# A provisional softmax bound for the first 512 keys of an attention block, with one input block transposed by DMA

## The chip, the cores and the metric

The kernel runs on one core of a Trainium2 chip. The metric is the device time of one execution in microseconds. A core has a matrix engine (TensorE, "PE" in the profile; its weight loads are "PEld"), a vector engine (VectorE, "DVE"), a scalar engine (ScalarE, "ACT"), GpSimd ("POOL") and SyncE ("SP"), which here only issues DMA transfers. DMA issues on the queue of an engine stand under "SPq" or "ACTq".

The profiled span is a little shorter than the reported time (413.1 against 415.36 us for the same execution of the kernel before). Reported times are compared with reported times, and points inside the span with points inside the span.

## The reference

```python
# x (1, 2048, 448), wqkv (448, 1344), wo (448, 448), all bf16;  H = 16 heads of Dh = 28
qkv = (x @ wqkv).reshape(B, S, 3, H, Dh).transpose(2, 0, 3, 1, 4)
q, k, v = qkv
scores = einsum("bhqd,bhkd->bhqk", q, k) * Dh ** -0.5
p = softmax(scores)
o = einsum("bhqk,bhkd->bhqd", p, v)
out = o.transpose(0, 2, 1, 3).reshape(B, S, D) @ wo
```

## The kernel before

**Shape of the work.** Four heads form a group, each padded from 28 to 32 rows of the 128 partitions. The queries come in chunks of 512. So there are 4 groups x 4 chunks = 16 windows; each window has 16 key tiles x 4 heads = 64 score tiles of 128 keys x 512 queries, 1024 in all. A score tile takes one matmul, then an exponential, and then one matmul into the value sums in the PSUM bank PO. Two engines make exponentials: ACT takes two tiles at once as one 128x1024 activation (848 tiles, 424 activations), and DVE with GpSimd takes 176 tiles with a polynomial (three DVE passes, one GpSimd pass).

**The bound.** Softmax needs something like the row maximum of the scores. The kernel uses an upper bound instead: the sum over d of |q_d| times the largest |k_d| over all keys. It comes out of the score matmul itself: next to the 32 rows of a head stand 32 more rows, which hold |q| on the query side (QB) and minus 1.03 times the maximum of |k| on the key side (KB). No exponential can start until the maximum over *all* 2048 keys is known, so until all four x blocks are loaded, transposed and projected to keys.

```python
    for b in range(NQC):                       # four x blocks of 512 rows
        nc.sync.dma_start(out=XS[b][:], in_=x_perm[:, b * TPC:(b + 1) * TPC, :])
    for (W, off) in ((WK, D), (WQ, 0)):
        nc.scalar.dma_start(out=W[:, :, 0:GW], in_=wq3[:, :, off:off + GW])
    ...
    for b in range(NQC):
        xs_in = add(Op("SP", 0.01, None, prio=-2000 + b, lat=(4.7, 6.1, 7.6, 9.0)[b]))
        for hf in range(2):
            ...
            tro = add(Op("PE", 0.55, tr, deps=[xs_in], ...))      # 8 transposes of 128x112 on TensorE
            evo = add(Op("DVE" if hf == 0 else "ACT", 0.6 if hf == 0 else 0.905, ev, deps=[tro], ...))
    ...
    def task_K(g, sc):                         # keys of block sc, group g
        ...
        if g == 0:
            red = ... tensor_reduce(out=KPART[g][:, sc:sc + 1], in_=ap(), op=ALU.max, apply_absolute_value=True)
            evs = [... nc.scalar.activation(out=KB[0][pr][:, cs], in_=ap(), func=ACT.Identity, bias=onescol[:, 0:1]) ...]
    def task_kmax(g):                          # maximum over the four blocks, then into the bound rows of KB
        m = ... tensor_reduce(out=KMAX[g][:], in_=KPART[g][:], op=ALU.max)
        ...
```

**The planner.** The kernel fixes the instruction order of each engine when it is built. A small event simulation in Python holds operations (`Op`: engine, assumed duration, assumed latency, dependencies, priority) and a handful of tuned constants, plays them through and emits the instructions in the order it finds. An engine then works through its list in that order. So an `Op("SP", 0.01, None, lat=4.7)` is an *assumption* that a load lands at 4.7 us. If it lands later on the chip, the result stays correct, but what stands behind its first user in that engine's order waits too: in the changed kernel below a block landed at 24.80 us where 13.0 was assumed, and score matmuls waited 8.9 us behind two projection matmuls that read it. The constants that matter below are `DI` (how many DVE tiles must be in work before output sums may go ahead of score matmuls near the end), `NTAIL` (DVE takes none of the last so many tiles), `UO` and `UQ` (how early a projection may take a bank from the score tiles), and `QEA`, `QPR`, `OD` for the order of the query projections.

## Time and profile before

The median of the three runs given with the kernel was 415.18 us (414.97 to 415.36).

| kernel before | us |
|---|---|
| first exponential starts | 16.38 |
| fourth exponential starts | 19.45 |
| last exponential ends | 405.56 |
| span ends | 413.1 |

From the page of the kernel before: its span, the busy time of each engine with its share of the span, and the chain of work that ended last, by engine.

```profile
span 413.1 us, 7525 instructions
PE 362.4 (88%) x2605; PEld 121.4 (29%) x2617; DVE 394.0 (95%) x696; ACT 400.0 (97%) x439; POOL 224.1 (54%) x203
ACT 86%; issue 8%; PE 2%; DMA 2%; DVE 1%; SPq 0%; DVEq 0%; ACTq 0%
```

ACT is busy for 97% of the span and makes up 86% of the chain that ended last: it bounds the kernel. DVE at 95% is close behind.

The timeline of ACT in the kernel before gives the start, in us from the start of the span, the length, and the instruction with the shapes written and read; in brackets stands the idle time before it and what ended that.

```profile
16.38 1.02 ACT L903 ACTIVATE PTA_131<-PA_198 128x1024 bf16<-128x1024 f32 x1 [0.25 <-PE PA_198 L631]
17.63 1.02 ACT L903 ACTIVATE PTA_132<-PA_199 128x1024 bf16<-128x1024 f32 x1 [0.23 <-PE PA_199 L631]
18.55 1.02 ACT L903 ACTIVATE PTA_133<-PA_198 128x1024 bf16<-128x1024 f32 x1
19.45 1.03 ACT L903 ACTIVATE PTA_134<-PA_199 128x1024 bf16<-128x1024 f32 x1
...
404.28 1.28 ACT L903 ACTIVATE PTA_145<-PA_199 128x1024 bf16<-128x1024 f32 x1
```

After the second exponential no line carries a bracket until the last one ends at 404.28 + 1.28 = 405.56. The 424 exponentials follow each other at 0.917 us. So the time is a start (16.4 us), a stretch of exponentials at full rate (389 us) and a tail (7.5 us).

The timeline of DVE in the kernel before shows what stands in the tail.

```profile
400.13 0.69 DVE L727 SCALAR_TENSOR_TENSOR PTD_162<-PD_200,DG_182 128x512 uint16<-128x512 f32 x1 [0.50 <-POOL DG_182 L714]
403.58 0.63 DVE L602 TENSOR_TENSOR XS_129<-PD_202,KB_0_91 128x448 bf16<-128x448 f32 x1 [2.76 <-PE PD_202 L598]
...
406.04 0.72 DVE L643 STREAM_TRANSPOSE DT<-PO 128x512 f32<-128x512 f32 x1
```

DVE's last polynomial tile is finished at 400.82, 4.7 us before ACT's last exponential, so the last normalisation (the transpose of PO into DT) can start at 406.04, 0.5 us after that exponential.

### The profile page before, as it was taken

The page shows a single profiled execution, that of the slowest core. Times are in us where ns is not written, and L with a number is a line of the kernel's source. Part 1 is how long each engine was busy: PE and PEld are TensorE (multiplying, and loading weights), DVE is VectorE, ACT ScalarE, POOL GpSimd, SP SyncE. Part 2 cuts the span into 40 slices and gives each one's busy share as a digit, 9 for nine tenths or more (in the row PEclk, how much of TensorE's full clock was granted, in tenths as well). Part 3 has the DMA queues.
Part 4 walks back from the last instruction along what each step waited for, and adds up shares of the span by engine and source line. Part 5 has one row for each costly group of instructions (what it writes and reads, how often), then busy time and mean ns, then how long its engine had stood idle before and what let it go on. Part 6 is the DMA issues. An engine that isn't in the chain of part 4 may idle for free.

```text
span 413.1 us, 7525 instructions
## 1 busy us (share of the span) xinstructions
PE 362.4 (88%) x2605; PEld 121.4 (29%) x2617; DVE 394.0 (95%) x696; ACT 400.0 (97%) x439; POOL 224.1 (54%) x203
## 2 busy tenths in 40 slices
PE   8988989898898889888898988979898888989995
PEld 4533232223232232322223222222322222222231
DVE  6899999999999999999999999999999999999975
ACT  4999999999999999999999999999999999999994
POOL 2155456464655556475465656547375656556450
PEclk9999999999999999999999999999999999999999
DMA  8410011202201001110400001010310101001012
GB/s 256 77 20 21 3 47 11 53 25 54 72 1 44 2 28 30 20 38 8 111 8 27 21 9 40 2 36 11 77 48 2 47 2 35 12 27 47 4 69 89
DMA packets 33413, 15.83 MB, mean 38 GB/s; under 512 B 26016, under 2 KB 30304, under 8 KB 33376
## 3 DMA queue, kind: packets, MB, share of 16 engines
q1 hardware_dynamic: 32304, 15.05, 14.5%
q8 instruction: 20, 0.33, 0.4%
q10 hardware_dynamic: 1072, 0.32, 0.3%
q14 instruction: 17, 0.14, 0.1%
HBM read 7.37 MB, written 1.96 MB: 23 GB/s over the span
## 4 chain that ended last, share of the span: by engine, by line
ACT 86%; issue 8%; PE 2%; DMA 2%; DVE 1%; SPq 0%; DVEq 0%; ACTq 0%
ACT PTA_131 L903 5%; ACT PTA_132 L903 4%; ACT PTA_133 L903 4%; ACT PTA_136 L903 4%; ACT PTA_135 L903 4%; ACT PTA_134 L903 4%; ACT PTA_145 L903 4%; ACT PTA_140 L903 4%; ACT PTA_139 L903 4%; ACT PTA_138 L903 4%; ACT PTA_137 L903 4%; ACT PTA_144 L903 4%; ACT PTA_142 L903 3%; ACT PTA_143 L903 3%; ACT PTA_141 L903 3%
## 5 line engine op out<-in xcount | busy, mean ns | idle before, releaser
L714 POOL TENSOR_TENSOR DG_181<-DV_175,DU_169 128x512 f16<-128x512 f16 x30 | 34.6, 1155 | 34.8 <-DVE DV_175 L711 34.6
L714 POOL TENSOR_TENSOR DG_182<-DV_176,DU_170 128x512 f16<-128x512 f16 x30 | 34.6, 1155 | 28.8 <-DVE DV_176 L711 28.7
L714 POOL TENSOR_TENSOR DG_184<-DV_178,DU_172 128x512 f16<-128x512 f16 x29 | 33.5, 1155 | 29.5 <-DVE DV_178 L711 28.2
L714 POOL TENSOR_TENSOR DG_186<-DV_180,DU_174 128x512 f16<-128x512 f16 x29 | 33.5, 1155 | 26.9 <-DVE DV_180 L711 26.7
L714 POOL TENSOR_TENSOR DG_185<-DV_179,DU_173 128x512 f16<-128x512 f16 x29 | 33.5, 1155 | 25.7 <-DVE DV_179 L711 25.6
L714 POOL TENSOR_TENSOR DG_183<-DV_177,DU_171 128x512 f16<-128x512 f16 x29 | 33.5, 1156 | 22.9 <-DVE DV_177 L711 22.7
L631 PEld LDWEIGHTS <-KB_1_94 64*128 64x128 bf16 x256 | 20.8, 92 | 48.4 <-issue 47.4
L631 PEld LDWEIGHTS <-KB_0_91 64*128 64x128 bf16 x256 | 20.5, 92 | 45.8 <-issue 42.1
L631 PEld LDWEIGHTS <-KB_1_92 64*128 64x128 bf16 x256 | 20.1, 93 | 45.8 <-issue 44.0
L631 PEld LDWEIGHTS <-KB_0_93 64*128 64x128 bf16 x256 | 20.3, 92 | 43.5 <-issue 42.5
L903 ACT ACTIVATE PTA_140<-PA_199 128x1024 bf16<-128x1024 f32 x18 | 22.4, 1247 | 0.0
L903 ACT ACTIVATE PTA_144<-PA_199 128x1024 bf16<-128x1024 f32 x18 | 22.4, 1245 | 0.0
L903 ACT ACTIVATE PTA_143<-PA_198 128x1024 bf16<-128x1024 f32 x18 | 22.3, 1241 | 0.0
L903 ACT ACTIVATE PTA_142<-PA_199 128x1024 bf16<-128x1024 f32 x18 | 22.3, 1239 | 0.0
L903 ACT ACTIVATE PTA_141<-PA_198 128x1024 bf16<-128x1024 f32 x18 | 22.3, 1236 | 0.0
L903 ACT ACTIVATE PTA_139<-PA_198 128x1024 bf16<-128x1024 f32 x17 | 21.1, 1241 | 0.0
L708 DVE TENSOR_SCALAR DU_171<-PD_202 128x512 f16<-128x512 uint16 x29 | 19.8, 682 | 1.0 <-PE PD_202 L631 0.7
L708 DVE TENSOR_SCALAR DU_172<-PD_200 128x512 f16<-128x512 uint16 x29 | 19.7, 681 | 0.9 <-PE PD_200 L631 0.9
L711 DVE SCALAR_TENSOR_TENSOR DV_178<-PD_200,DU_172 128x512 f16<-128x512 uint16 x29 | 19.8, 684 | 0.3
L711 DVE SCALAR_TENSOR_TENSOR DV_176<-PD_201,DU_170 128x512 f16<-128x512 uint16 x29 | 19.8, 683 | 0.2
L708 DVE TENSOR_SCALAR DU_169<-PD_200 128x512 f16<-128x512 uint16 x29 | 19.8, 682 | 0.2 <-PE PD_200 L631 0.2
L903 ACT ACTIVATE PTA_145<-PA_198 128x1024 bf16<-128x1024 f32 x16 | 20.0, 1247 | 0.0
(596 smaller groups left out, 1511.3 us busy)
## 6 DMA issues: line engine op xcount, KB each, us to landing
RRB_194<-SCR_196 SPq DMA_DIRECT2D x8, 256.0 KB
RRB_195<-SCR_197 SPq DMA_DIRECT2D x7, 256.0 KB
KB_1_94<-KB_0_93 SPq DMA_DIRECT2D x4, 128.0 KB
XS_127<-in_x_dram SPq DMA_DIRECT2D x1, 448.0 KB
XS_128<-in_x_dram SPq DMA_DIRECT2D x1, 448.0 KB
XS_129<-in_x_dram SPq DMA_DIRECT2D x1, 448.0 KB
XS_130<-in_x_dram SPq DMA_DIRECT2D x1, 448.0 KB
out_dram<-XS_127 SPq DMA_DIRECT2D x1, 448.0 KB
```

The source lines that it names most:

```text
L631: nc.tensor.matmul(out=ap, lhsT=KB[g % 2][i // 2][a:a + 64, j * P:(j + 1) * P], rhs=QB[w % NQB][i // 2][a:a + 64, :], start=True, stop=Tru ...
L708: p1 = add(Op("DVE", P1, lambda: nc.vector.tensor_scalar(out=DU[b][:], in0=lo, scalar1=SIG / 65536, scalar2=SIG * (SS - 0.5), op0=ALU.mult ...
L711: p2 = add(Op("DVE", P1, lambda: nc.vector.scalar_tensor_tensor(out=DV[b][:], in0=lo, scalar=65536 * (SS - 0.5 + CE / C3), in1=DU[b][:], o ...
L714: gq = add(Op("POOL", PTT, lambda: nc.gpsimd.tensor_tensor(out=DG[b][:], in0=DV[b][:], in1=DU[b][:], op=ALU.mult), deps=[p2], prio=n, kind ...
L903: nc.scalar.activation(out=PTA[pslot.idx][:, 0:len(ns) * QW], in_=PA[s.idx][:, 0:len(ns) * QW], func=ACT.Exp, bias=ACT_BIAS, scale=ACT_SCALE)
```

## The change

The intent is to start the exponentials earlier. The first 512 keys of the first window get a bound of their own, from the maximum of their own block. Only x block 0, WK and WQ are needed for it. The other 1536 keys of that window use the bound of all keys, as before. The two partial value sums then stand on different bases: the first is multiplied by the exponential of the difference of the bounds (8 small matmuls, one 128x512 activation on ACT, one multiplication on GpSimd) and added to the second at the end of the window.

Four further parts go with it:
- For group 0 the maximum moves from the key side to the query side (a DVE multiplication for each query chunk), and the keys of blocks 1 to 3 are copied to their places by eight DMA moves.
- Constants are made on GpSimd, which is idle for 6.38 us up to 8.75 in the trace of the kernel before, and partly on DVE. WQ goes to the sync queue right after x block 0, and WO is loaded later.
- One of the four x blocks (rows 8 to 11 of every 16) is not transposed on TensorE any more but loaded by 16 transposing DMAs of 128x128.
- The planner's constants are set anew.

The diff, cut to its core (most of it left out, marked by `...`):

```diff
-    DI = 2
+    DI = 1
-    QEA = 30
+    QEA = 20
-    UQ = 16
-    OD = 4
+    UQ = 30
+    OD = 2
-    UO = 40
+    UO = 20
+    FB = TPC
+    XLAT = (4.45, 6.9, 8.3, 9.6)
+    WQLAT = 5.9
+    XT3 = 13.0
+    T0 = (0, 4, 12, 8)
...
+    nc.scalar.dma_start(out=WK[:, :, 0:GW], in_=wq3[:, :, D:D + GW])
     for b in range(NQC):
-        nc.sync.dma_start(out=XS[b][:], in_=x_perm[:, b * TPC:(b + 1) * TPC, :])
-    for (W, off) in ((WK, D), (WQ, 0)):
-        nc.scalar.dma_start(out=W[:, :, 0:GW], in_=wq3[:, :, off:off + GW])
+        if b < NQC - 1:
+            nc.sync.dma_start(out=XS[b][:], in_=x_perm[:, T0[b]:T0[b] + TPC, :])
+        if b == 0:
+            nc.sync.dma_start(out=WQ[:, :, 0:GW], in_=wq3[:, :, 0:GW])
     nc.sync.dma_start(out=WV[:], in_=wq3[:, :, 2 * D:3 * D])
+    for cc in range(CC):
+        for t in range(TPC):
+            nc.sync.dma_start(out=XT[NQC - 1][cc // 2][:, cc % 2, t * P:(t + 1) * P],
+                              in_=bass.AP(x.tensor, x.offset + (T0[NQC - 1] + t) * D + cc * CK, [[NKT * D, P], [1, P]]),
+                              transpose=True)
...
+    xt_done[NQC - 1].append(add(Op("SP", 0.01, None, prio=-1996, lat=XT3)))
+    add(Op("SP", 10.2, None, prio=-1995.5))
...
+            b0 = []
             for i in range(HG):
...
+                o = bound(qb, i, KPART[0], [ab, kmaxop[0][0], e1], -4370 + 0.01 * i if i < 2 else -4350 + 0.01 * i)
+                b0.append(o)
                 qev[(g, c, i)] = [o]
+            for i in range(HG):
+                qev2[i] = bound(q2, i, KMAX[0], [cps[i // 2], ab, kmax_op[0]], -4000 + 0.01 * i)
...
-                         rhs=QB[w % NQB][i // 2][a:a + 64, :], start=True, stop=True, tile_position=(a, 0))
+                         rhs=QB[2 if w == 0 and j >= FB else w % NQB][i // 2][a:a + 64, :], start=True, stop=True, tile_position=(a, 0))
...
+    def task_factor():
+        ...
+        e = add(Op("ACT", 0.49, lambda: nc.scalar.activation(out=DT[:], in_=bank(task)[:], func=ACT.Exp, scale=ACT_SCALE),
+                   deps=[m], prio=0))
...
+    def finish_block():
+        pvop = rows[(0, FB - 1)]["pv"]
+        ev = add(Op("DVE", 0.62, lambda: nc.vector.tensor_copy(out=RRB[1][:], in_=PO[:]), deps=[pvop], prio=-5000))
+        ...
+        first_part.append(add(Op("POOL", 1.22, lambda: nc.gpsimd.tensor_tensor(out=RRB[1][:], in0=RRB[1][:], in1=DT[:], op=ALU.mult),
+                                 deps=[ev, factor], prio=-10, kind="n")))
```

`XT3 = 13.0` and the 10.2 below it are the planner's assumptions about the transposing DMAs: all landed at 13.0 us, the sync queue busy until about 10.2 us. The 10.2 count from the start of the simulation, because the operations before it on that queue take 0.01 us each.

## The prediction

One sentence is cut out of the text below, where marked. It was no term of the forecast's sum (net 2.2 to 2.7 us, 412.5 us), which stands in full.

> **What bounds the kernel now.** ScalarE (ACT). By the page, ACT is busy 97% of the 413.1 us span, VectorE (DVE) 95%; the chain that ended last is 86% ACT, nearly all 128x1024 exponentials. By the timeline the first exponential starts at 16.38, and from the second on ACT has no idle gap until the last ends at 405.56: 424 exponentials in 389.2 us, 0.917 apart. The other 176 score tiles take three DVE passes and one GpSimd pass each. So the time is 16.4 us of start, 389 of exponentials, 7.5 of tail.
>
> **What sets the 16.4 us.** By the timeline: WQ is padded only from 8.75 (GpSimd, 1.33 us); four x blocks are transposed on TensorE and copied by ACT (1.0 us) and DVE (0.69 us); four key projections, four DVE maxima (0.69 us) and the overall maximum (14.21) precede the bound; the query is projected last (13.2), evacuated at 14.29; bounds and absolute values end at 15.8.
>
> **What the change does.** The first 512 keys need only x block 0, WK, WQ and their own maximum. ACT loses two copies (1.0 us each) before the first exponential and evacuates query and keys sooner; two key evacuations move to after the third exponential. One x block comes by 16 transposing DMAs from the sync queue. GpSimd makes constants in idle time. The instruction orders show the same 424 exponentials and 176 DVE tiles, so the 389 us term stays.
>
> Estimate from trace durations: x block 0 lands about 4.6, is transposed and copied by 7.1; query and key matmuls end by 8.7; ACT query evacuation to 9.6; DVE absolute value, copy, x-copy (0.69) and two bounds (0.72) end near 11.5; first exponential near 12.0, 4.4 us earlier. Given back on ACT later: two key evacuations (0.59 us pitch, 1.2 us), one 128x512 exponential for the factor (0.5 us), and a 0.5 us gap before the second exponential (one buffer, second pair of bounds). Net 2.2 to 2.7 us. Added DVE work after the start (three multiplies of 0.25, one 0.68 us evacuation, more bounds) is off the chain, but DVE has only a few us of idle between 17 and 400.
>
> **Prediction: 412.5 us, 80% range 410.3 to 414.6.** Faster by over 2%: 0.03; within 2%: 0.95; slower by over 2%: 0.02.
>
> **What would show it.** Timeline: first exponential at 11.5 to 12.8; the fourth (before: 19.45) near 16.5; spacing 0.917 afterwards; the last ending 2 to 3 us earlier; tail about 7.5 us. ACT waits under 1 us in total after the third exponential.
>
> **What would make it wrong.**
> - TensorE, in order, meets key block 3's matmuls before the second to fifth score groups. No DMA transpose is in this trace; if the last lands after about 15 us, every later exponential shifts. The kernel's plan assumes 13.0.
> - The eight moves of keys 512 to 2047 by DMA: an issue took 0.63 us before, and a tile waited until 1.6 us after the last issue. [...] My estimate: first needed about 20 us, the first four landing by 20: little slack, a 1 us stall is possible.
> - DVE starting its tiles later (near 19 against 17.35) with more work: if the balance tips, ACT or the tail waits.
> - Faster than I think: data lands earlier, or the retuned tail order saves some of the 7.5 us.

## The result, and the profile after

| | median us | lowest to highest | runs |
|---|---|---|---|
| before | 415.08 | 414.57 to 415.36 | 4 |
| after | 425.94 | 425.65 to 426.47 | 4 |

The ratio is 1.0268 (95% interval 1.0253 to 1.0282): slower. A ratio here and below is not quite the ratio of the medians that are quoted.

From the page of the changed kernel: span, busy times and the chain that ended last.

```profile
span 424.5 us, 7553 instructions
PE 361.5 (85%) x2593; PEld 121.0 (28%) x2606; DVE 396.6 (93%) x703; ACT 397.6 (94%) x436; POOL 229.0 (54%) x222
ACT 79%; issue 6%; PE 5%; SPq 5%; DVE 2%; DMA 1%; DVEq 0%
```

The engines do nearly the same work as before (ACT even 2.4 us less), but the span is 11.4 us longer: this is waiting. The new member of the chain is "SPq" with 5%, the issuing of DMAs on the sync queue.

The timeline of ACT in the changed kernel:

```profile
12.00 1.04 ACT L1047 ACTIVATE PTA<-PA 128x1024 bf16<-128x1024 f32 x1
13.54 1.94 ACT L1047 ACTIVATE PTA<-PA 128x1024 bf16<-128x1024 f32 x2 [0.49 <-PE PA L729]
15.86 0.69 ACT L467 ACTIVATE KB<-PD,onescol 128x512 bf16<-128x512 f32 x1 [0.38 <-DVE KPART L454]
26.28 0.69 ACT L467 ACTIVATE KB<-PD,onescol 128x512 bf16<-128x512 f32 x1 [9.74 <-DVE KPART L454]
26.87 3.83 ACT L1047 ACTIVATE PTA<-PA 128x1024 bf16<-128x1024 f32 x4
31.83 1.02 ACT L1047 ACTIVATE PTA<-PA 128x1024 bf16<-128x1024 f32 x1 [1.13 <-PE PA L729]
```

The first exponential starts at 12.00, 4.4 us earlier than before. Three run, and then ACT waits 9.74 us to evacuate the keys of the last x block. The line puts the wait down to DVE's maximum of that block (KPART), but DVE was itself idle for 9.73 us just then, waiting for the projection. So one looks one step further back, at the timeline of PE in the changed kernel:

```profile
15.07 0.39 PE L729 MATMUL PA<-QB,KB 64*128 64x512 bf16 x2
19.72 0.61 PE L447 MATMUL PD<-XT,WKP 112*128 112x512 bf16 x1 [4.26 <-DMA XT<-in_x_dram]
24.93 0.59 PE L447 MATMUL PD<-XT,WKP 112*128 112x512 bf16 x1 [4.60 <-DMA XT<-in_x_dram]
25.45 0.61 PE L729 MATMUL PA<-QB,KB 64*128 64x512 bf16 x2
```

In PE's order the last two matmuls of that projection (L447) stand between the score matmuls (L729). Each waits for transposed pieces of x, 8.9 us together, and the scores behind them wait too, although nothing that the next ones read is missing (e_true below ran five exponentials in this time). And the timeline of the sync queue in the changed kernel shows why the pieces are late:

```profile
3.20 20.48 SPq L235 DMA_TRANSPOSE XT<-in_x_dram  x16
```

The 16 transposing DMAs need from 3.20 to 23.68 only to be *issued*, 1.28 us apart. The chain shows the last one issued at 22.45 and landed 2.35 us later, at 24.80, where the plan had 13.0.

The windows view of the changed kernel adds the granted TensorE clock. After the stretch come its length, busy time and number of instructions for PE, PEld, DVE, ACT and POOL, then the clock, the DMA share and GB/s.

```profile
17.00:21.40 4.40, 0.61 (x1) 0.11 (x1) 0.00 (x0) 0.00 (x0) 0.00 (x0) 0.64 0.14 25
21.40:38.00 16.60, 11.04 (x80) 5.16 (x81) 10.99 (x21) 10.58 (x12) 3.38 (x3) 0.79 0.30 43
```

In the first of these stretches, inside TensorE's wait, its granted clock averages 0.64, and it averages 0.79 over the 16.6 us after that. Narrower windows of the same view show 1.00 from 15.46 to 18.00, 0.60 from 18 to 19, 0.50 from 19 to 28, 0.78 from 28 to 29 and 1.00 from 29 to 32, so the clock halved near 18.2 and came back near 28.4. The fall came about 2.7 us after the last matmul before the wait had ended (15.46), the return about 3.5 us after work resumed at 24.93. What decides these times was not shown.

The end of the changed kernel, in DVE's timeline and then in PE's:

```profile
413.29 0.68 DVE L861 SCALAR_TENSOR_TENSOR PTD<-PD,DG 128x512 uint16<-128x512 f32 x1
...
417.31 0.72 DVE L743 STREAM_TRANSPOSE DT<-PO 128x512 f32<-128x512 f32 x1 [2.27 <-PE PO L900]
```

```profile
414.33 1.88 PE L764 MATMUL PD<-WO,OT 128*128 128x448 bf16 x9
...
416.36 0.82 PE L900 MATMUL PO<-PTA,VA 128*32 128x512 bf16 x12
```

The last exponential ends at 414.73. DVE's last tile is finished at 413.97, only 0.76 us before it (4.7 us before, in the kernel before). Nine matmuls of the output projection stand in front of the last value matmuls, and the final normalisation starts at 417.31, 2.6 us after the last exponential instead of 0.5.

So the 11.4 us of longer span are, term by term:

| part of the span, us | before | after | difference |
|---|---|---|---|
| start to first exponential | 16.38 | 12.00 | -4.38 |
| first to fourth exponential | 3.07 | 14.87 | +11.80 |
| fourth exponential to the end of the last | 386.11 | 387.86 | +1.75 |
| end of the last exponential to the end | 7.54 | 9.77 | +2.23 |
| sum | 413.1 | 424.5 | +11.4 |

The 1.75 is made of the wait of 1.13 at 31.83 (score matmuls that wait for the key moves by DMA), 0.47 for the factor's activation (it starts at 43.59 in the same timeline, the next exponential at 44.06), and 0.15 that was not assigned.

### The profile page after: what moved, and what is told of

It is laid out like the page before. It is cut to its first block, busy times and chain, and to the rows that moved or that the text cites. A ratio compares the mean times of both kernels' runs of the same rounds, so it can differ in the third digit from the quotient of the medians.

```text
span 424.5 us, 7553 instructions
## 1 busy us (share of the span) xinstructions
PE 361.5 (85%) x2593; PEld 121.0 (28%) x2606; DVE 396.6 (93%) x703; ACT 397.6 (94%) x436; POOL 229.0 (54%) x222
## 4 chain that ended last, share of the span: by engine, by line
ACT 79%; issue 6%; PE 5%; SPq 5%; DVE 2%; DMA 1%; DVEq 0%
ACT PTA L1047 79%; SPq L235 4%; PE PA L729 2%; PE PO L900 1%; DMA KB<-KB 1%; DMA XT<-in_x_dram 1%; PE PO L550 0%; PE PD L764 0%; DVE DV L845 0%; PE PD L729 0%; SPq L229 0%; SPq L496 0%; DVE DU L842 0%; PE PO L447 0%; ACT OUTF L1176 0%
## 5 line engine op out<-in xcount | busy, mean ns | idle before, releaser
L1047 ACT ACTIVATE PTA<-PA 128x1024 bf16<-128x1024 f32 x424 | 389.5, 1252 | 1.6 <-PE PA L729 1.6
L848 POOL TENSOR_TENSOR DG<-DV,DU 128x512 f16<-128x512 f16 x176 | 202.3, 1153 | 176.7 <-DVE DV L845 169.0
L729 PE MATMUL PA<-QB,KB 64*128 64x512 bf16 x848 | 167.4, 381 | 44.3 <-ACT PTA L1047 40.4
L842 DVE TENSOR_SCALAR DU<-PD 128x512 f16<-128x512 uint16 x176 | 118.6, 680 | 3.5 <-PE PD L729 3.2
L729 PEld LDWEIGHTS <-KB 64*128 64x128 bf16 x1024 | 67.2, 93 | 186.0 <-issue 178.8
L845 DVE SCALAR_TENSOR_TENSOR DV<-PD,DU 128x512 f16<-128x512 uint16 x176 | 118.8, 681 | 1.1
L861 DVE SCALAR_TENSOR_TENSOR PTD<-PD,DG 128x512 uint16<-128x512 f32 x176 | 119.0, 678 | 0.6 <-POOL DG L848 0.2
L900 PE MATMUL PO<-PTA,VA 128*32 128x512 bf16 x848 | 85.6, 386 | 0.0
L729 PE MATMUL PD<-QB,KB 64*128 64x512 bf16 x176 | 65.1, 379 | 1.1 <-DVE PTD L861 0.4
L900 PE MATMUL PO<-PTD,VA 128*32 128x512 bf16 x176 | 58.1, 387 | 0.0
L447 PE MATMUL PO<-XT,WKP 112*128 112x512 bf16 x48 | 15.0, 385 | 0.1
L447 PE MATMUL PD<-XT,WKP 112*128 112x512 bf16 x16 | 5.4, 407 | 9.3 <-DMA XT<-in_x_dram 8.9
L454 DVE TENSOR_REDUCE KPART<-PD 128x1 f32<-128x512 f32 x4 | 2.8, 690 | 10.4 <-PE PD L447 10.3
L447 PEld LDWEIGHTS <-WKP 112*128 112x128 bf16 x64 | 4.6, 97 | 18.6 <-issue 13.3
```

Of the source, the lines that this page charges most:

```text
L447: ops = chain_mm(CC, lambda cc: nc.tensor.matmul(out=ap(), lhsT=WKP[g][:, cc, :], rhs=XT[sc][cc // 2][0:CK, cc % 2, :], start=(cc == 0), s ...
L729: nc.tensor.matmul(out=ap, lhsT=KB[g % 2][i // 2][a:a + 64, j * P:(j + 1) * P], rhs=QB[2 if w == 0 and j >= FB else w % NQB][i // 2][a:a + ...
L842: p1 = add(Op("DVE", P1, lambda: nc.vector.tensor_scalar(out=DU[b][:], in0=lo, scalar1=SIG / 65536, scalar2=SIG * (SS - 0.5), op0=ALU.mult ...
L845: p2 = add(Op("DVE", P1, lambda: nc.vector.scalar_tensor_tensor(out=DV[b][:], in0=lo, scalar=65536 * (SS - 0.5 + CE / C3), in1=DU[b][:], o ...
L848: gq = add(Op("POOL", PTT, lambda: nc.gpsimd.tensor_tensor(out=DG[b][:], in0=DV[b][:], in1=DU[b][:], op=ALU.mult), deps=[p2], prio=n, kind ...
L861: f = add(Op("DVE", P1, lambda: nc.vector.scalar_tensor_tensor(out=PTD[st["s"].idx][:].bitcast(U16), in0=PX[slot.idx][:], scalar=EBITS + C ...
```

## The experiments

**Theory**: the change loses because of the transposing DMAs. They are too many instructions for one queue, the plan believed that they land at 13.0, and everything behind their first user in PE's order waits. The gain of 4.4 us at the start is real. **Rival 1**: the new structure (bounds on the query side, key moves, factor, a second pass over PO) loses time by itself and would be slower with any loading of x. **Rival 2**: it is not the DMAs but the wrong plan; told the truth, the planner would find other work for the wait. Later a third question came up: what makes the tail longer. The expectations below name their alternatives each in its own words; where one speaks of a theory and a rival by letter or name, it means those stated in that text.

All kernels gave correct results. Times are medians in us. The kernel before had 414.78 (7 runs) in the rounds of the first four rows, 414.79 (7 runs) in those of the next four, and 414.95 (9 runs) in those of the last three.

| label | what it is | median | ratio (95%) |
|---|---|---|---|
| e_pe | change, last x block transposed on TensorE | 426.57 | 1.0284 (1.0269 to 1.0300) |
| e_before_dt | kernel before with the 16 transposing DMAs | 428.94 | 1.0347 (1.0324 to 1.0371) |
| e_big | change, 4 transposing DMAs instead of 16 | 415.60 | 1.0019 (1.0002 to 1.0036) |
| e_true | change, planner told the measured landing | 431.45 | 1.0400 (1.0384 to 1.0415) |
| e_pe2 | as e_pe, other bank for one transpose | 416.10 | 1.0029 (1.0014 to 1.0043) |
| e_after_di | change, only `DI` set back | 425.74 | 1.0263 (1.0245 to 1.0281) |
| e_big_di | e_big, `DI` set back | 414.65 | 0.9996 (0.9981 to 1.0011) |
| e_mid | change, 8 transposing DMAs | 415.52 | 1.0014 (0.9998 to 1.0031) |
| e_after_tail | change, two tiles fewer on DVE, `UO` set back | 424.82 | 1.0245 (1.0231 to 1.0260) |
| e_best | e_big with the tail of e_after_tail | 414.40 | 0.9987 (0.9974 to 1.0001) |
| e_pe_best | e_pe2 with its own tail | 414.34 | 0.9989 (0.9976 to 1.0002) |

### e_before_dt: the transposing DMAs alone, in the kernel before

```diff
+    XT3 = 13.0
+    T0 = (0, 4, 12, 8)
...
-    for b in range(NQC):
-        nc.sync.dma_start(out=XS[b][:], in_=x_perm[:, b * TPC:(b + 1) * TPC, :])
+    for b in range(NQC - 1):
+        nc.sync.dma_start(out=XS[b][:], in_=x_perm[:, T0[b]:T0[b] + TPC, :])
...
+    for cc in range(CC):
+        for t in range(TPC):
+            nc.sync.dma_start(out=XT[NQC - 1][cc // 2][:, cc % 2, t * P:(t + 1) * P], ..., transpose=True)
```

> The kernel before with only the 16 transposing DMAs put in for x block 3. Theory: the last transposed piece lands at 24.8, the first exponential moves from 16.4 to about 28 to 29.5, total 426 to 430 us. Rival (the transposing DMAs are harmless, the early bound is to blame): within 2 us of 415.

Measured: 428.94, a ratio of 1.0347; the DMAs alone cost 14 us, without any early bound. The timeline of ACT in this kernel:

```profile
25.89 0.69 ACT L399 ACTIVATE KB<-PA,onescol 128x512 bf16<-128x512 f32 x1 [11.57 <-DVE KPART L396]
28.99 3.77 ACT L914 ACTIVATE PTA<-PA 128x1024 bf16<-128x1024 f32 x4 [2.40 <-PE PA L642]
```

The first exponential moved from 16.38 to 28.99, with the same wait for the last key block. The total lies inside the expected 426 to 430, as the theory has it; rival 1 has no place for it. It is more than the change lost, because here no exponential can start before the last block has come.

### e_big and e_mid: fewer and larger transposing DMAs

The rows of a block are made consecutive in memory (the views of x and of the output change along), so that one DMA can transpose 512 or 256 rows. The diff of e_big against the changed kernel:

```diff
     for cc in range(CC):
-        for t in range(TPC):
-            nc.sync.dma_start(out=XT[NQC - 1][cc // 2][:, cc % 2, t * P:(t + 1) * P],
-                              in_=bass.AP(x.tensor, x.offset + (T0[NQC - 1] + t) * D + cc * CK, [[NKT * D, P], [1, P]]),
-                              transpose=True)
+        nc.sync.dma_start(out=XT[NQC - 1][cc // 2][:, cc % 2, :],
+                          in_=bass.AP(x.tensor, x.offset + T0[NQC - 1] * P * D + cc * CK, [[D, QW], [1, P]]),
+                          transpose=True)
```

e_mid takes two DMAs of 256 rows for each `cc`; apart from that it is e_big:

```diff
+        for hv in range(2):
+            nc.sync.dma_start(out=XT[NQC - 1][cc // 2][:, cc % 2, hv * 256:(hv + 1) * 256],
+                              in_=bass.AP(x.tensor, x.offset + (T0[NQC - 1] * P + hv * 256) * D + cc * CK, [[D, 256], [1, P]]),
+                              transpose=True)
```

> The change, but 4 transposing DMAs of 512 rows by 128 columns instead of 16 of 128 by 128 (rows of a block made contiguous so that one instruction can take them). Theory A (issue costs about 1.28 us per instruction): last landing near 9.5, fourth exponential near 16.5, total about 415 to 416 (the tail of the change, 2.2 us longer, stays). Theory B (issue costs per 128x128 piece, about 5 us per instruction): last landing near 25, total within 1.5 us of 425.9.

> Half-way dose: 8 transposing DMAs of 256 rows by 128 columns. Issue per instruction was 1.28 us at 128 rows and 1.8 us at 512, so 1.4 to 1.5 is expected here (mostly a cost per instruction), the queue free near 15, last landing near 16, fourth exponential at 18 to 19.5, total 416 to 418. If the cost were per byte: last landing near 25 and 425; but then 4 instructions would have cost that as well.

Measured: 415.60 and 415.52; e_big lies inside its expected range, e_mid just below its own. The three kernels asked for the line of their transposing DMAs (duration of one issue in ns as minimum/median/maximum, and the first and last start in us), first the changed kernel:

```profile
L235 SPq DMA_TRANSPOSE XT<-in_x_dram x16: 1215/1232/1352, 3.2 to 22.4; - x16
```

e_mid:

```profile
L235 SPq DMA_TRANSPOSE XT<-in_x_dram x8: 1240/1242/2244, 3.1 to 12.7; - x8
```

e_big:

```profile
L234 SPq DMA_TRANSPOSE XT<-in_x_dram x4: 1260/1720/2542, 3.1 to 9.3; - x4
```

An issue of 128 rows and one of 256 rows take the same 1.24 us (median), so in this range the cost goes by instruction and not by byte. At 512 rows the four issues of e_big took, in order, 2.54, 1.34, 2.10 and 1.26 us; the same four instructions took 1.91, 1.26, 1.39 and 1.26 in e_big_di. So the shortest issue is hardly longer than one of 128 rows, and the median of four says little. In e_mid too, the first and the last issue were longer than the rest (1.83 and 2.24). Whether the excess comes of the size or of a wait is not shown. The queue is free at 23.68 with 16 pieces, at 14.98 with 8, and at 10.53 with 4. In e_big nothing waits for the transposed block, in e_mid a matmul waits 0.7 us. One caution: the rows of a piece are 16 rows apart in memory in the changed kernel and consecutive in e_mid and e_big; e_mid's equal issue time speaks against that being the cause, but the two were not varied separately.

The timeline of ACT in e_big, to be held against that of the changed kernel:

```profile
12.69 1.04 ACT L1046 ACTIVATE PTA<-PA 128x1024 bf16<-128x1024 f32 x1
...
17.45 0.69 ACT L466 ACTIVATE KB<-PD,onescol 128x512 bf16<-128x512 f32 x1 [0.22 <-DVE KPART L453]
18.03 4.67 ACT L1046 ACTIVATE PTA<-PA 128x1024 bf16<-128x1024 f32 x5
```

The wait of 9.74 is now 0.22, and the fourth exponential starts at 18.03. (The first is 0.7 us later than in the changed kernel. In this execution x block 1 landed later: its transposes, which stand in PE's order before the query's projection, began at 7.68 against 7.00. In e_big_di, with the same start, the first exponential was at 11.67.) The change in the medians from 425.94 to 415.60 puts the price of the small pieces at 10.3 us. The theory holds for the main term. (e_mid's last piece landed at 16.14 and its fourth exponential started at 17.92, no later than in e_big, so its total is no worse either.) But e_big is not faster than the kernel before: the interval lies just above 1, so a rest was to be explained.

### e_pe and e_pe2: the last x block transposed on TensorE

Both take the transposing DMAs out and treat the fourth x block like the others. They differ in the PSUM bank of the block's first transposed half. e_pe:

```diff
-             ((PA[0][:, 0:QW], None), (PA[0][:, QW:2 * QW], None)), ())
+             ((PA[0][:, 0:QW], None), (PA[0][:, QW:2 * QW], None)), ((PO[:], 3), (PA[0][:, 0:QW], 4)))
...
-    open_when(o_slot, [xt_half[3]])
+    open_when(o_slot, [xt_half[6]])
```

> The change, but x block 3 loaded plainly and transposed on TensorE as before; early bound, rescaling and constants kept. Theory (the transposing DMAs on the sync queue cost the time: 16 issues of 1.28 us, last landing at 24.8): first exponential near 12, the fourth near 17 instead of 26.87, no wait over 1.5 us on ScalarE after it; total 411 to 414.5 us. Rival (the early bound with its second accumulation, factor, extra DVE passes and key moves costs the time): at least 420 us.

Measured: 426.57, as slow as the change. Taken alone this would have spoken for rival 1. The trace says otherwise. The start is good (the first exponential at 12.32, and no wait for a transposed block), but ACT's timeline shows a new wait later, where the first window ends:

```profile
48.16 2.85 ACT L1040 ACTIVATE PTA<-PA 128x1024 bf16<-128x1024 f32 x3 [8.28 <-PE PA L722]
```

and PE's timeline shows the cause:

```profile
38.75 1.04 PE L543 MATMUL PD<-XT,WQP 112*128 112x512 bf16 x4
```

The query projection for the next window (L543) gets a bank only at 38.75, when the scores of the first window have run out. Its result must still be evacuated and moved by DMA before a score of the next window can start, and PE's next score matmul comes at 46.77. The planner, with slightly changed timing, had starved the projection; there is another such wait of 3.63 us at 388. So e_pe was decided by an accident of the order and does not answer the question. e_pe2 was made to ask it again, with the bank PD2 for that half:

```diff
-             ((PA[0][:, 0:QW], None), (PA[0][:, QW:2 * QW], None)), ())
+             ((PA[0][:, 0:QW], None), (PA[0][:, QW:2 * QW], None)), ((PD[2][:], 2), (PA[0][:, 0:QW], 4)))
...
-    k0_wait = [lambda: [xt_half[0]], lambda: quse, lambda: kuse[0], lambda: [xt_half[2]]]
+    k0_wait = [lambda: [xt_half[0]], lambda: quse, lambda: kuse[0], lambda: [xt_half[6]]]
```

> As e_pe (early bound kept, x block 3 loaded plainly and transposed on TensorE), but its first transposed half in another PSUM bank, so that the planner no longer starves the second window's query (in e_pe that query's matmuls came at 38.75 and ScalarE then waited 8.3 us). Theory (transposing DMAs cost the 10 us; e_pe lost through order alone): first exponential near 12.3, the fourth near 17, no ScalarE wait over 1 us later, total 412.5 to 416. Rival (the early bound itself costs): 420 or more again.

Measured: 416.10, just above what the theory gave and far from the 426 of the change. The timeline of ACT in e_pe2:

```profile
11.66 1.04 ACT L1040 ACTIVATE PTA<-PA 128x1024 bf16<-128x1024 f32 x1
13.35 1.02 ACT L1040 ACTIVATE PTA<-PA 128x1024 bf16<-128x1024 f32 x1 [0.64 <-PE PA L722]
...
15.16 2.84 ACT L1040 ACTIVATE PTA<-PA 128x1024 bf16<-128x1024 f32 x3
```

With the same structure and no transposing DMA the stall is gone. Rival 1, in the form that the structure is what costs ten microseconds, is out. e_big and e_pe2, with quite different ways of loading, lie 0.5 us apart.

### e_true: the planner told what was measured

```diff
-    XT3 = 13.0
+    XT3 = 24.9
...
-    add(Op("SP", 10.2, None, prio=-1995.5))
+    add(Op("SP", 23.7, None, prio=-1995.5))
```

> The change, with only the planner's assumed landing of the transposes set from 13.0 to the measured 24.9 and the sync queue busy until 23.7; same work, other order. Theory (latency itself costs most, order a part): four more exponentials run during the wait, but then TensorE and ScalarE still wait for block 3 because the full maximum needs it; 419 to 423 us. Rival (only the wrong order costs; right order hides the wait): 413 or less.

Measured: 431.45, slower still, which neither theory nor rival 2 had. Early on the planner did what rival 2 hoped: five exponentials ran between 16.78 and 21.4, inside the former wait. Two waits were left there (4.53 and 2.92 us). But the new plan starved a query projection again, this time that of the last window, and one line of ACT's timeline takes back more than was won:

```profile
395.99 2.85 ACT L1047 ACTIVATE PTA<-PA 128x1024 bf16<-128x1024 f32 x3 [8.21 <-PE PA L729]
```

So a true assumption is not enough: the constants of this planner are tuned to one set of landings, and any shift can open an 8 us hole hundreds of microseconds later. As a test of rival 2 the run stays inconclusive; it only shows that the plan's order can fill part of the wait (5 exponentials, about 4.6 us), and that even then ACT waited another 4.53 us for the keys of the last block.

### e_after_di, e_big_di, e_after_tail: the tail

The tail is 9.77 us in the change, 9.91 in e_big and 9.61 in e_pe2, against 7.54 before. First suspect: `DI = 1`, which lets output sums go ahead of score matmuls already when one DVE tile is in work. One constant set back, in the change and in e_big:

```diff
-    DI = 1
+    DI = 2
```

> The change with DI back at 2, nothing else: in the instruction order six of the nine late output sums then come after the last value matmuls instead of before. Theory (the 2.2 us longer tail comes of that order): the last transpose of the sums on VectorE starts 0.6 to 1.2 us after the last exponential ends instead of 2.6, total 423.9 to 424.6. Rival (the tail is long because of the late start): no change, 425.9.

> Both repairs: 4 transposing DMAs of 512 rows, and DI 2. If the two causes are separate they add: 415.6 minus 1.5 to 2.0, so 413.5 to 414.2, a little under the kernel before (414.8).

Measured: 425.74 and 414.65, both above their expected ranges. The tail became 9.29 and 9.24 us: about half a microsecond, where 2 were expected. The timeline of DVE in e_after_di, whose last exponential ends at 413.71:

```profile
414.77 1.15 DVE L700 TENSOR_TENSOR XS<-PD,KB 128x448 bf16<-128x448 f32 x2 [1.81 <-PE PD L696]
415.85 0.70 DVE L743 STREAM_TRANSPOSE DT<-PO 128x512 f32<-128x512 f32 x1
```

Now DVE's own output additions (L700) stand before the normalisation, which still starts 2.1 us after the last exponential. So `DI` was not the cause; output sums still stand in the way. The second suspect was the balance: DVE finishes its tiles too late, and what has to follow piles up at the end. So DVE gets less: its last tile must lie four tiles earlier, and the output projection may take a bank earlier again.

```diff
-    NTAIL = 12
+    NTAIL = 16
...
-    UO = 20
+    UO = 40
```

> The change with its 16 small transposing DMAs, but VectorE tiles stop 4 tiles earlier (NTAIL 16) and UO back at 40: one exponential more on ScalarE (425), two VectorE tiles fewer, and in the instruction order all but two of the four late output sums of window 2 come before the last scores are done. Theory (in the change VectorE runs behind, its last tile 0.8 us before the last exponential against 4.7 before, and so the output sums fall into the tail): last exponential about 0.5 to 0.9 later, VectorE's transpose of the sums starts 0.5 to 0.8 us after it instead of 2.6, tail 7.6 to 8.0 instead of 9.8, total 424.3 to 425.0. Rival (tail is given by the order of late sums alone, as in e_after_di): 425.5 or more.

Measured: 424.82, inside the expected range. ACT now makes 425 exponentials and DVE 174 tiles. The timeline of DVE:

```profile
410.87 0.69 DVE L861 SCALAR_TENSOR_TENSOR PTD<-PD,DG 128x512 uint16<-128x512 f32 x1 [0.42 <-POOL DG L848]
...
417.10 0.72 DVE L743 STREAM_TRANSPOSE DT<-PO 128x512 f32<-128x512 f32 x1
```

The normalisation starts 0.56 us after the last exponential (416.54), and the tail is 7.66 us, as in the kernel before. The price is one more exponential on ACT. (The profiled execution also has waits of ACT, 1.6 us in four places between 30 and 39 us. It was the slowest of its four, 426.21 against 424.53 to 424.83, so these waits need not be in the others; e_best, with the same two constants and no late transposes, has none there.)

The edit changes two constants that were not varied apart, and e_pe2 speaks against the balance alone. It too has 425 exponentials and 174 tiles, with the old `NTAIL = 12` and `UO = 20`. Its DVE timeline, with the last exponential ending at 404.39:

```profile
397.29 0.69 DVE L854 SCALAR_TENSOR_TENSOR PTD<-PD,DG 128x512 uint16<-128x512 f32 x1 [0.73 <-POOL DG L841]
...
403.67 0.62 DVE L696 CAST XS<-PD 128x448 bf16<-128x448 f32 x1 [5.16 <-PE PD L689]
...
406.77 0.70 DVE L736 STREAM_TRANSPOSE DT<-PO 128x512 f32<-128x512 f32 x1
```

DVE's last tile is done 6.4 us before the last exponential, and DVE then waits 5.16 us for output sums; still the normalisation comes 2.4 us late and the tail is 9.61. Fewer tiles on DVE are therefore not enough. Nor are the new constants needed: e_pe and e_true, with the old ones, have tails of 7.9 and 7.7 us, but there ACT waited (3.63 and 8.21 us) shortly before the end. What the late kernels share is that, after the last exponential, output sums stand in front of the normalisation, on PE (the changed kernel) or on DVE (e_after_di, e_pe2). In the kernel's code `UO` also decides from which tile on output sums may go ahead of score matmuls, which makes it the likelier of the two constants; that is not shown.

### e_best and e_pe_best: the change at its best, with and without transposing DMAs

e_best is e_big with the two constants of e_after_tail. e_pe_best is e_pe2 with `NTAIL = 14`, `UO = 40` and some further constants of the tail, chosen by building variants and looking at the planner's order, without running them. Its diff against e_pe2:

```diff
-    NTAIL = 12
-    JL = 6
-    JACC = 8
+    NTAIL = 14
+    JL = 4
+    JACC = 9
-    J3 = 9
+    J3 = 10
-    SPLIT = {2: (0, 1, 2, 3), 3: (2,)}
-    ACCQ = (0, 1, 3)
+    SPLIT = {2: (0, 1, 2, 3), 3: (1, 2)}
+    ACCQ = (0, 3)
-    UO = 20
+    UO = 40
```

e_best's diff against e_big:

```diff
-    NTAIL = 12
+    NTAIL = 16
-    UO = 20
+    UO = 40
```

> Large transposing DMAs with the same tail repair: first exponential 11.7 to 12.7, fourth near 17, tail 7.6 to 8.0; total 413.3 to 414.2, so 0.1 to 0.4 percent under the kernel before. If the repairs do not add: 415 or more.

> No transposing DMA at all (as e_pe2) with the tail planned anew: total 413.3 to 414.5. Tells whether the transposing DMA is worth having at all once it is issued in large pieces: if this equals e_best within 0.5 us, it is worth nothing.

Measured: 414.40 and 414.34, against 414.95 for the kernel before; e_best lies 0.2 us above its expected range, e_pe_best inside its own. Both ratios are 0.999 with intervals that just touch 1: the same, with a gain of about 0.1% likely and not quite shown. The timelines of e_best, of ACT and of DVE:

```profile
11.96 1.04 ACT L1046 ACTIVATE PTA<-PA 128x1024 bf16<-128x1024 f32 x1
...
17.30 5.59 ACT L1046 ACTIVATE PTA<-PA 128x1024 bf16<-128x1024 f32 x6
```

```profile
399.11 0.69 DVE L860 SCALAR_TENSOR_TENSOR PTD<-PD,DG 128x512 uint16<-128x512 f32 x1 [0.42 <-POOL DG L847]
...
405.33 0.72 DVE L742 STREAM_TRANSPOSE DT<-PO 128x512 f32<-128x512 f32 x1
```

e_best shows where the 4.4 us of earlier start go when nothing stalls:

| part of the span, us | before | e_best | difference |
|---|---|---|---|
| start to first exponential | 16.38 | 11.96 | -4.42 |
| first to fourth exponential | 3.07 | 5.34 | +2.27 |
| fourth exponential to the end of the last | 386.11 | 387.48 | +1.37 |
| tail | 7.54 | 7.62 | +0.08 |
| sum | 413.1 | 412.4 | -0.7 |

The 2.27 are the two key evacuations, which ACT did before the first exponential in the kernel before and now does between the third and the fourth, with small waits for DVE around them (0.37 and 0.22), and a longer wait before the second exponential (0.49 against 0.23). In the 1.37 the factor's activation and one more exponential can be named (0.5 and 0.9 us). And the two kernels agree to 0.06 us with and without transposing DMAs, so in this kernel the transposing DMA brings nothing even when it is issued in large pieces.

## Why the prediction was wrong, point by point

- **What bounds the kernel** (ACT; start + exponentials + tail): right. It made the decomposition possible, and the sums close.
- **"first exponential near 12.0, 4.4 us earlier"**: right, 12.00, and 11.66 to 12.69 in the experiments that start the same way.
- **"the fourth (before: 19.45) near 16.5"**: wrong, 26.87. This is the step that failed: the landing of the last x block was taken over from the kernel's plan ("The kernel's plan assumes 13.0"). The runs showed 24.80. Named as a risk ("if the last lands after about 15 us, every later exponential shifts"), it was left out of the range. In the plan the queue is free at about 10.2 us; counted from the first transposing issue (3.20 in the trace of the changed kernel) that leaves 7.0 us for 16 pieces, 0.44 us each, the size of a plain issue on that queue in the kernel before (0.38 to 0.65 us at the start). Measured were 1.28 us from issue to issue. So the plan in effect priced an instruction that the trace had never shown like one that it had. The issues themselves took 1.23 us each in the profile (median; 1.215 to 1.352). In the kernel before, one plain issue of 0.38 to 0.65 us sufficed for each whole x block (448 KB); the last block took 16 transposing issues and 20.5 us in the changed kernel, which is 24 GB/s from the first issue at 3.20 to the last landing at 24.80 (524,288 bytes written), and the 4 large issues of e_big still took 7.4 us. The chance of slower, 0.02, was far too small for a duration that nothing in the trace had measured.
- **With the stall away, the fourth exponential** was at 17.3 (e_best) and 17.0 (e_big_di): 0.5 to 0.8 us later than predicted (in e_big, with its later start, 18.0). Two small waits of ACT for DVE's maxima (0.37 and 0.22 us in e_best) were not in the sum.
- **The stall for the key moves**, "a 1 us stall is possible": right, 1.13 us in the changed kernel; but none in e_big and e_best, where the moves are issued from 17.25 and 16.52 in place of 26.02. Nor is there one in e_after_di, where they are issued from 25.81 but take 5.58 us to issue instead of 6.30.
- **From issue to landing**: the last transposing piece landed 2.35 us after its issue began and 1.12 us after its issue ended. That is not where the time went. The time went into the issuing.
- **"tail about 7.5 us"**: wrong, 9.77. The second mis-sized term, by 2.2 us. The prediction named a risk of it ("if the balance tips, ACT or the tail waits") but did not price it. With two tiles fewer on DVE and the earlier claim on a bank together (e_after_tail, e_best) the tail is 7.6 us. e_after_di showed that the most obvious constant is not the reason, and e_pe2 that two tiles fewer are not enough. In all late kernels output sums stood before the last normalisation; which decision of the planner put them there stays open.
- **Net gain of 2.2 to 2.7 us**: in no run. The best versions gained about 0.6 us in the medians. The prediction took the tail as unchanged and the 424 exponentials as kept. No measured version of the change had both: those with 424 exponentials had a tail of 9.2 to 9.9 us, and those with a tail of 7.6 to 7.9 us had one or two exponentials more on ACT, at 0.9 us each (e_pe2 had one more and the long tail as well). Whether that must be so, because DVE has no room for the added work, is not shown.

Left open: why a transposing issue takes at least 1.2 us at each size tried (128, 256 and 512 rows), and some of the larger ones up to 2.54; what lengthens the tail; whether another share of tiles between ACT and DVE would keep more of the gain; and the 0.15 us not assigned. Sharing the pieces between two queues was not tried.

## What to carry to other kernels

A constant in a kernel's own schedule is an assumption, and where a change brings in an instruction that no trace has yet measured, its price belongs in the range: here sixteen transposing issues on one queue took 20.5 us, sixteen times the 1.28 us from one to the next. Where a kernel fixes the order of each engine, as this one does, look for what stands *behind* the first user of a late load; here score matmuls waited 8.9 us behind two projection matmuls, and those of five exponentials were ready (e_true). And an earlier start is worth only what is not given back: in e_best, of 4.4 us, 2.3 went to work and waits moved behind the start, 0.5 to the correction factor, 0.9 to one more exponential, and 0.7 was kept.
